# Attention products turned round: v as the stationary operand, 64-row score products, and maxima read straight from PSUM

## The chip, the cores and the metric

The program runs on one core of one Trainium2 chip, as one launch. The metric is the device time of one execution in microseconds. A core has five instruction queues: TensorE (matmuls, written PE in the profile, its weight loads PEld), VectorE (DVE), ScalarE (ACT), GpSimd (POOL) and SyncE (SP), which mostly issues DMAs. Each queue runs its instructions in order; semaphores hold one queue until another has done its part.

## The reference

Attention with rotary position encoding over 4 batches, 8 heads, 576 positions and 64 dimensions, then a mixture of 8 experts with one expert for each of 2304 tokens, then a dense feed-forward layer. The change touches the attention alone:

```
q_rot, k_rot = rotate(q), rotate(k)
scores = (1 / sqrt(64)) * q_rot @ k_rot.T          # 32 times 576 x 576
scores = scores - max(scores, over keys)
attn = exp(scores);  attn = attn / (sum(attn, over keys) + 1e-9)
out = attn @ v                                     # 576 x 64 for each head
x = out, heads side by side: 2304 x 512            # input of the experts
```

All inputs and outputs are fp32.

## The kernel before

**Pairs of heads.** The 32 heads are handled as 16 pairs, `p` = 0 to 15, four pairs to a batch. Head `e` (0 or 1) of a pair has its 64 dimensions on partitions 64e to 64e+63. `load` brings q and k, `rope` rotates them (six tensor operations a pair, on GpSimd except where `OFF` names them for VectorE), `hi` and `lo` split each rotated value into two 16-bit halves, and `stack` lays the halves out by DMA so that 128 rows hold both halves of one head.

**Scores twice.** `sc` (L279) multiplies queries (stationary) with keys (moving) for the row maximum: eight tiles of 128 queries, four for each head, and a ninth that holds the last 64 queries of both heads. A tile has 576 columns in two PSUM banks of 288. ScalarE copies one bank to SBUF (L294), and VectorE scans it against the other bank, so that the last element is the maximum (`sc_max`, L305). `m_split` (L319, L329) negates the maxima into a small matrix, `m_turn` (L335 to L341) turns it by two matmuls, copies it out and writes it by two DMAs from SP's queue into the stacked operands as one more row. `st` (L351, L352) then computes the scores again, transposed (keys on partitions, queries along the columns), with that row taking the maximum off, in two matmuls for each of two column blocks. `exp` (L354) writes the nine tiles to `P`, in fp32.

**Product with v.** `p_lo` (L360) subtracts from each fp32 weight its upper 16 bits, read in place as bf16, which gives a lower half in fp16; some tiles do this on GpSimd, as `OFF['pool...']` lists, the others on VectorE. `pv` (L375 to L377) has the weights as stationary operand (128 keys x 128 queries) and v as the moving one: 64 columns, and a column of 0.25 whose product is the row sum. Three products of halves for each of five key blocks and five query blocks and two heads make 150 matmuls a pair. Each head has an accumulator bank of its own (`obank`, two in turn). `epi` (L386 to L399) adds 1e-9, inverts the sum and multiplies. `v_load`, `v_hi` and `v_lo` bring and split v once a batch. `r_hi`, `r_lo` and the functions after them route the result to the experts.

**Buffers.** Six PSUM banks are three pairs (`pair`, L140), given out in turn to `sc`, `st`, `m_turn` and the router's products. Before a pair is given out again, `Turns` emits the maximum that is still to read it (L136).

**Order.** Every function is entered with a due time (`add`, L60); `emit` sorts all by it, and that is the order of each engine's instructions. A pair of heads is nine units apart from the next (`z = 9 * p`, one unit for each `st` tile). `sc` of a pair runs 15.7 units ahead of its first `st`, `m_turn` about 5 ahead, `pv` from 10.4 to 18.5 units behind. `OFF` holds small shifts of these due times by function, tile and pair. The expert visits start at unit 144.6, while pair 15 is at unit 135 to 154.

Of the kernel before, what the change touches and what calls it, by code (L numbers as in the profile page):

```python
# [44 lines left out]
def kernel(ctx: ExitStack, tc: tile.TileContext, qk, vp, cs, cf, tid, emb, tau, w1, w2, wi, wo, out, tag=None):  # L45
# [63 lines left out]
    for name, size in (  # L109
# [3 lines left out]
    ):  # L113
        off[name], top = top, top + size
# [14 lines left out]
    class Turns:  # L129
# [62 lines left out]
    qkt, hlt, mtp, pt, ot, xt, vh, vl, v32 = ({} for _ in range(9))  # L192
# [37 lines left out]
    def v_load(b, g):  # L230
        v32[b, g] = v32t()
        nc.sync.dma_start(out=v32[b, g].rearrange("p a d -> p (a d)"), in_=vp[b][:, 576 * g:576 * g + 576])

    def v_hi(b, g):
        if g == 0:
            vh[b] = at(f"v{b % 2}", F16, 36, 65)
            vl[b] = at(f"v{b % 2}", F16, 36, 64, add=4704)
            nc.gpsimd.memset(vh[b][:, :, 64:65], 0.25)
        nc.scalar.activation(vh[b][:, 9 * g:9 * g + 9, 0:64], v32[b, g], AF.Copy, scale=64.0)

    def v_lo(b, g):
        r = slice(9 * g, 9 * g + 9)
        nc.vector.scalar_tensor_tensor(vl[b][:, r], v32.pop((b, g)), 64.0, vh[b][:, r, 0:64], op0=ALU.mult, op1=ALU.subtract)
# [29 lines left out]
    def warm(n):  # L273
        t = bank(obank(), 512)
# [4 lines left out]
    def sc(p, i):  # L279
        after(("stack", p))  # L280
        d = D4[p % 4]
        t = pair()
        for c in OFF.get('c1', (0, 1)):
            cc = slice(288 * c, 288 * c + 288)
            if i < 8:
                e, q0 = i // 4, (i % 4) * 128
                nc.tensor.matmul(t[:, c, 0:288], lhsT=d[:, e, 0, q0:q0 + 128], rhs=d[:, e, 2, cc], start=True, stop=True)  # L287
            else:
                for e in range(2):
                    nc.tensor.matmul(t[64 * e:64 * e + 64, c, 0:288], lhsT=d[:, e, 0, 512:576], rhs=d[:, e, 2, cc], start=True, stop=True)  # L290
        m = sE[(9 * p + i) % 15]
        sct[p, i] = t
        pair.due[(pair.n - 1) % 3] = p, i
        nc.scalar.copy(m, t[:, 1, 0:288])  # L294

    sE = [at("et", F16, 288, add=576 * s) for s in range(15)]
    sct = {}

    def sc_max(p, i):
# [3 lines left out]
        m = sE[(9 * p + i) % 15]  # L303
# [3 lines left out]
    def m_split(p, i):  # L307
        mv = at("et", F16, 15, 288)[:, :, 287]
        mh = MH1[p % 2]
        after(*[("sc_max", p, k) for k in (range(4), range(4, 8), (8,), ())[i]])  # L310

        def put(c, s, n):
            while n:
                s %= 15
                k = min(n, 15 - s)
                if p in OFF.get('msA', ()):
                    nc.scalar.activation(mh[:, c:c + k], mv[:, s:s + k], AF.Copy, scale=-1.0)
                else:
                    nc.vector.tensor_scalar(mh[:, c:c + k], mv[:, s:s + k], -1.0, None, op0=ALU.mult)  # L319
                c, s, n = c + k, s + k, n - k  # L320

        if i == 0:
            put(0, 9 * p, 4)
        elif i == 1:
            put(5, 9 * p + 4, 4)
        elif i == 2:
            put(4, 9 * p + 8, 1)
        else:
# [950 lines left out]
```

## Time and profile before

| | |
|---|---|
| median of 3 runs | 1074.34 us (1073.21 to 1080.97) |
| the profiled execution | 1081.06 us |
| its span, first to last instruction | 1079.2 us |
| TensorE busy, share of the span | 900.1 us, 83% |
| VectorE | 809.6 us, 75% |
| GpSimd | 607.7 us, 56% |
| ScalarE | 549.6 us, 51% |
| mean granted TensorE clock | 0.91 |

The span is one execution on the chip. A matmul's busy time holds its drain, which overlaps the next matmul, so a busy TensorE need not be at its peak; what a matmul costs in a row of them is the distance of the starts. The granted clock is 1.00 at 2.4 GHz and 0.5 at 1.2 GHz; a stretch's figure is the mean. Attention fills the first third of the span, the experts and the feed-forward layer the rest, so shares over the whole span say little on attention.

### The profile page before, as it was taken

Reading aid. Unit: us, or ns where it says so; the run is one execution under the profiler, and the core shown is the slowest. Engines: PE = TensorE matmul, PEld = TensorE weight load, DVE = VectorE, ACT = ScalarE, POOL = GpSimd, SP = SyncE. Lnnn points to the kernel's source line nnn. Section 1 sums busy time; section 2 is a strip of 40 time slices with the busy share of each in tenths; the row PEclk is TensorE's granted clock in tenths of the full one; section 3 lists DMA queues with packets and bytes.
Section 4 is the critical chain, followed back from the end, with each engine's and each line's share of the span. In section 5 each row is a group of like instructions: output and inputs, shape, how many; then the busy total and the mean of one; then the engine's idle time right before and its main releaser. Section 6 shows DMA issues by size and latency. Waiting matters only on the chain. (4 is left out here: it accounts for less than half of the span.)

```text
span 1079.2 us, 25502 instructions
## 1 busy us (share of the span) xinstructions
PE 900.1 (83%) x9622; PEld 702.8 (65%) x9622; DVE 809.6 (75%) x1265; ACT 549.6 (51%) x982; POOL 607.7 (56%) x665
## 2 busy tenths in 40 slices
PE   2577788777788899899968897369899999999994
PEld 1255556545566687677645573258688888888884
DVE  8898998999986846666899887896656656655751
ACT  2454564546455633555776544544555555554540
POOL 6585685677543713233234655567667757657650
PEclk8588887889798989899989998699899999999998
DMA  6644337446342744979999655210112022012000
GB/s 222 187 133 133 89 94 165 153 125 127 104 108 50 227 101 139 297 209 284 327 319 281 194 144 157 81 41 11 50 40 60 21 41 60 21 41 60 21 20 20
DMA packets 128426, 133.73 MB, mean 124 GB/s; under 512 B 67736, under 2 KB 104600, under 8 KB 128288
## 3 DMA queue, kind: packets, MB, share of 16 engines
q1 hardware_dynamic: 119648, 103.75, 35.8%
q0 software_dynamic: 8352, 27.62, 7.8%
q8 instruction: 78, 1.28, 0.5%
q10 hardware_dynamic: 288, 0.59, 0.2%
q14 instruction: 60, 0.49, 0.1%
HBM read 86.36 MB, written 16.17 MB: 95 GB/s over the span
## 5 line engine op out<-in xcount | busy, mean ns | idle before, releaser
L1047 PE MATMUL banks<-arena 128*128 128x256 f16 x576 | 160.1, 278 | 30.9 <-ACT arena L1062 25.9
L1048 PE MATMUL banks<-arena 128*128 128x256 f16 x576 | 160.2, 278 | 0.0
L1049 PE MATMUL banks<-arena 128*128 128x256 f16 x576 | 160.1, 278 | 0.0
L354 ACT ACTIVATE arena<-banks 128x576 f32<-128x576 f32 x144 | 93.4, 652 | 115.2 <-PE banks L352 114.9
L1082 DVE TENSOR_TENSOR arena<-arena 128x896 f16<-128x896 f32 x72 | 80.2, 1114 | 88.8 <-ACT arena L1078 84.1
L1099 PE MATMUL banks<-arena 128*128 128x256 f16 x504 | 138.1, 274 | 4.0 <-DVE arena L1114 4.0
L1100 PE MATMUL banks<-arena 128*128 128x256 f16 x504 | 138.2, 274 | 0.0
L1101 PE MATMUL banks<-arena 128*128 128x256 f16 x504 | 138.2, 274 | 0.0
L967 PE MATMUL banks<-arena 128*128 128x128 f16 x704 | 125.9, 225 | 9.6 <-DVE arena L940 7.3
L965 PE MATMUL banks<-arena 128*128 128x128 f16 x704 | 126.1, 225 | 8.7 <-DMA arena<-arena 8.7
L1078 ACT ACTIVATE arena<-arena 128x896 f16<-128x896 f32 x71 | 67.5, 950 | 127.8 <-POOL arena L1075 124.3
L966 PE MATMUL banks<-arena 128*128 128x128 f16 x704 | 126.1, 225 | 0.0
L305 DVE TENSOR_TENSOR_SCAN arena<-banks,arena 128x288 f16<-128x288 f32 x144 | 106.5, 747 | 19.2 <-ACT arena L294 18.2
L377 PE MATMUL banks<-arena 128*128 128x65 f16 (+1 forms) x800 | 114.5, 202 | 6.9 <-DVE arena L360 6.1
L375 PE MATMUL banks<-arena 128*128 128x65 f16 (+1 forms) x800 | 115.8, 205 | 0.0
L360 POOL TENSOR_TENSOR arena<-arena 128x576 f16<-128x576 f32 x48 | 65.2, 1362 | 89.6 <-ACT arena L354 80.6
L376 PE MATMUL banks<-arena 128*128 128x64 f16 (+1 forms) x800 | 115.1, 202 | 0.0
L351 PE MATMUL banks<-arena 128*128 128x288 f16 (+1 forms) x320 | 89.1, 319 | 20.3 <-DVE arena L305 17.1
L1072 POOL TENSOR_TENSOR arena<-arena 128x256 f32<-128x256 f32 x67 | 54.5, 813 | 86.7 <-DVE arena L1069 86.7
L360 DVE TENSOR_TENSOR arena<-arena 128x576 f16<-128x576 f32 x96 | 96.0, 1004 | 2.4 <-ACT arena L354 2.4
L375 PEld LDWEIGHTS <-arena 128*128 128x128 bf16 (+1 forms) x800 | 80.0, 103 | 25.4 <-issue 10.1
L287 PE MATMUL banks<-arena 128*128 128x288 f16 x256 | 65.3, 333 | 32.7 <-DVE arena L305 23.7
(236 smaller groups left out, 2737.3 us busy)
## 6 DMA issues: line engine op xcount, KB each, us to landing
arena<-in_w_dram SPq DMA_DIRECT2D x64, 512.0 KB
arena<-in_qk_dram SPq DMA_DIRECT2D x30, 576.0 KB
arena<-in_wi_dram SPq DMA_DIRECT2D x16, 512.0 KB
arena<-in_wo_dram SPq DMA_DIRECT2D x32, 256.0 KB
arena<-arena SPq DMA_DIRECT2D x32, 216.0 KB
xreg<-arena POOLq DMA_DIRECT2D x25, 260.0 KB, 4.3
arena<-in_vp_dram SPq DMA_DIRECT2D x16, 288.0 KB
arena<-arena SPq DMA_DIRECT2D x32, 144.0 KB
```

The source lines that it names most:

```text
L360: eng.tensor_tensor(PLO[:, r], P32[:, r], PHB[:, r], op=ALU.subtract)
L375: nc.tensor.matmul(o[:, qt, :], lhsT=PHB[r, q], rhs=vh[b][r, vi], start=kt == 0, stop=False)
L376: nc.tensor.matmul(o[:, qt, 0:64], lhsT=PHB[r, q], rhs=vl[b][r, vi], start=False, stop=False)
L965: nc.tensor.matmul(o[:, fc], lhsT=w[:, 0, a], rhs=x[:, k], start=k == 0, stop=False)
L966: nc.tensor.matmul(o[:, fc], lhsT=w[:, 0, a], rhs=x[:, 4 + k], start=False, stop=False)
L967: nc.tensor.matmul(o[:, fc], lhsT=w[:, 1, a], rhs=x[:, k], start=False, stop=k == 3)
L1047: nc.tensor.matmul(o[:, v], lhsT=wih[k][:, f0:f0 + 128], rhs=z[:, :, k], start=k == 0, stop=False)
L1048: nc.tensor.matmul(o[:, v], lhsT=wih[k][:, f0:f0 + 128], rhs=z[:, :, 4 + k], start=False, stop=False)
L1049: nc.tensor.matmul(o[:, v], lhsT=wil[k][:, f0:f0 + 128], rhs=z[:, :, k], start=False, stop=k == 3)
L1099: nc.tensor.matmul(y, lhsT=a, rhs=b, start=u + f + n == 0, stop=False)
L1100: nc.tensor.matmul(y, lhsT=a, rhs=w[:, 1, WB[i - 1]], start=False, stop=False)
L1101: nc.tensor.matmul(y, lhsT=q[:, 1, f, GB[i - 1]], rhs=b, start=False, stop=u + f == 4 and n == len(m) - 1)
```

## The change

- The **score products** for the maximum (`sc`) contract over 64 rows, the upper halves of q and k alone, instead of 128. The tiles of the two heads are computed in one call, matmul by matmul in turn, from rows 0 to 63 and 64 to 127.
- The **maximum** (`sc_max`) is one reduction over both banks, negated, written straight into the small matrix. The copy by ScalarE and three of the four parts of `m_split` are gone.
- `m_turn`'s two DMAs are issued by ScalarE's queue instead of SP's.
- **`pv`** has v as the stationary operand, 64 columns for each head, so that head 0 writes PSUM partitions 0 to 63 and head 1 partitions 64 to 127; the weights are the moving operand, 576 queries in blocks of 256 and 320. Key blocks 0, 1 and 2 (`KF`) are multiplied in fp32; blocks 3 and 4 (`KH`) in three products of halves as before. The row sums come from a stationary of 32 columns of 0.25, in four strips of 32 partitions, in what is left of the two banks. The work is cut by key blocks, and each is due while the pair's `st` still runs.
- `p_lo` is left with tiles 3, 7 and 8; of these 3 and 8 are on GpSimd and 7 on VectorE, for every pair.
- Both heads share the two accumulator banks. `o_out` copies them to SBUF, `o_turn` turns them by eight fp32 transposes into a `pair`, and `epi` reads from there, for both heads at once.
- v is loaded in five parts a batch instead of four; three stay in fp32 in place, two are split.
- Due times: `pv` runs 3.6 to 10.9 units behind the first `st`, and what follows a pair (`y`) 12.9 instead of 19.6. The order of `st` tiles alternates between the heads. In `OFF`, the shifts of `p_lo`, `pv`, `epi`, `m_split`, `m_turn`, `v_hi`, `v_lo` and `sc_max` and the lists `pool1` to `pool15` and `poolz` are gone. `r_acc_t` and `r_acc` are now also emitted before their PSUM pair is given out again, and the router of batch 2 is due 10.2 instead of 7.2 units after `y`.

```diff
+    KF, KH = (0, 1, 2), (3, 4)
+    LT = [4 * e + kt for kt in KH if kt < 4 for e in range(2)] + [8]
-    obank = Turns([banks[:, 6], banks[:, 7]])
+    obank = banks[:, 6:8]
...
-    def sc(p, i):
+    def sc(p, n):
...
+            for e in range(2):
+                a, ce = slice(64 * e, 64 * e + 64), c if n < 4 else (c + e) % 2
+                o = two[e][:, ce, 0:288] if n < 4 else two[e][a, ce, 0:288]
+                nc.tensor.matmul(o, lhsT=d[a, e, 0, q0:q0 + (128 if n < 4 else 64)], rhs=d[a, e, 2, 288 * ce:288 * ce + 288], start=True, stop=True)
-        nc.scalar.copy(m, t[:, 1, 0:288])
...
-        nc.vector.tensor_tensor_scan(m, t[:, 0, 0:288], m, -3e38, op0=ALU.max, op1=ALU.max)
+        nc.vector.tensor_reduce(out=MH1[p % 2][:, c:c + 1], in_=t[:, :, 0:288], op=ALU.max, axis=AX.XY, negate=True)
...
-        nc.sync.dma_start(out=d[64:65, 0, 1], in_=ms[0:5])
-        nc.sync.dma_start(out=d[0:1, 1, 1], in_=ms[5:10])
+        nc.scalar.dma_start(out=d[64:65, 0, 1], in_=ms[0:5])
+        nc.scalar.dma_start(out=d[0:1, 1, 1], in_=ms[5:10])
...
+    def pv(p, kt):
...
+        if kt in KF:
+            w = [vm[i2][:, KF.index(kt), 2 * (p % 4) + e] for e in range(2)]
+            terms = [[(w[e], P32[:, (9 * p + tiles[e][0]) % RP]) for e in range(2)]]
+            ones = [[(one32, P32[:, (9 * p + tiles[e][0]) % RP]) for e in range(2)]]
+        else:
...
+                for t, x in zip(terms, ((h, ph), (h, pl), (l, ph))):
+                    t.append(x)
+                for t, x in zip(ones, (ph, pl)):
+                    t.append((one16[a], x))
+        for c in range(2):
+            for n, t in enumerate(terms):
+                for e in range(2):
+                    w, x = t[e]
+                    nc.tensor.matmul(o[64 * e:64 * e + 64, c, 0:QC[c].stop - QC[c].start], lhsT=w, rhs=x[:, QC[c]], ...)
+        for c in range(2):
+            q0, m = QS[c]
+            for n, t in enumerate(ones):
+                for e in range(2):
+                    w, x = t[e]
+                    for h in range(2):
+                        r = 64 * e + 32 * h
+                        nc.tensor.matmul(o[r:r + 32, c, 512 - m:512] if c else o[r:r + 32, c, 256:384], lhsT=w, rhs=x[:, q0 + 128 * h:q0 + 128 * h + m], ...)
+    def o_out(p):
+        s = osb[p % 2]
+        nc.scalar.copy(s[:, 0, 0:384], obank[:, 0, 0:384])
+        nc.scalar.copy(s[:, 1], obank[:, 1])
+    def o_turn(p):
...
+        for k, a in enumerate((0, 128, 512, 640, 768, 256, 832, 960)):
+            nc.tensor.transpose(t[:, k], s[:, a:a + 128], cft[:, 0:128])
...
+            nc.vector.tensor_tensor(x, t[:, 0:5]..., ert.pop(p).to_broadcast([128, 5, 2, 64]), op=ALU.mult)
...
+        for n in range(5):
+            add(u + w * 2 * n, sc, p, n)
...
+            add(z + i, st, p, 4 * (i % 2) + i // 2 if i < 8 else 8)
+        for kt, t in zip(PVO, (3.6, 5.5, 7.5, 9.6, 10.9)):
+            add(z + t, pv, p, kt)
+        add(z + 11.3, o_out, p)
+        add(z + 12.6, o_turn, p)
...
-        b, y = p // 4, z + 19.6
+        b, y = p // 4, z + 12.9
```

## Rows read from the trace of the kernel before

**Rows 1.** The exponentials' line: count, duration ns min/median/max, first and last start.

```profile
L354 ACT ACTIVATE arena<-banks x144: 624/651/693, 44.4 to 372.2; 128x576 f32<-128x576 f32 x144
```

**Rows 2.** Stretches: busy us and instructions of each engine, granted clock, DMA share, GB/s.

```profile
107.00:329.00 222.00, 175.02 (x2296) 126.74 (x2294) 206.50 (x348) 120.86 (x263) 143.85 (x101) 0.85 0.45 117
329.00:372.00 43.00, 40.62 (x664) 31.54 (x661) 33.73 (x89) 27.24 (x53) 22.07 (x21) 0.92 0.51 145
372.00:405.00 33.00, 28.55 (x443) 24.45 (x441) 17.66 (x29) 11.73 (x24) 9.98 (x7) 0.90 0.54 123
...
800.00:840.00 40.00, 40.00 (x369) 35.85 (x367) 23.58 (x33) 20.85 (x36) 29.51 (x43) 1.00 0.15 41
```

**Rows 3.** Waits, 107 to 329: who waited for whom, us, times, longest.

```profile
ACT arena L354 <- PE banks L352: 73.8, 68, 5.4
PE banks L335 <- DVE MH L319: 17.2, 10, 2.9
```

**Rows 4.** Groups on TensorE, 107 to 329: busy us, mean ns, idle before, releaser.

```profile
L351 PE MATMUL banks<-arena 128*128 128x288 f16 x161 | 49.8, 320 | 11.7 <-DVE arena L305 10.3 <-DMA arena<-arena 0.6 <-DVE r L386 0.6
L287 PE MATMUL banks<-arena 128*128 128x288 f16 x170 | 42.5, 321 | 8.4 <-DVE arena L305 8.1
```

**Rows 5.** Groups on VectorE, 107 to 329.

```profile
L305 DVE TENSOR_TENSOR_SCAN arena<-banks,arena 128x288 f16<-128x288 f32 x97 | 72.2, 748 | 12.5 <-ACT arena L294 12.2
L360 DVE TENSOR_TENSOR arena<-arena 128x576 f16<-128x576 f32 x63 | 61.7, 981 | 0.0
...
L243 DVE SCALAR_TENSOR_TENSOR arena<-arena 128x576 f16<-128x576 f32 x10 | 15.5, 1550 | 0.0
L319 DVE TENSOR_SCALAR MH<-arena 128x4 f16<-128x4 f16 x17 | 11.6, 682 | 0.0
...
L399 DVE TENSOR_TENSOR arena<-banks,r 128x320 f32<-128x320 f32 x20 | 9.8, 490 | 0.6
```

**Rows 6.** Groups on ScalarE: copies of scores, 107 to 329; a 512-column PSUM read.

```profile
L294 ACT CAST arena<-banks 128x288 f16<-128x288 f32 x97 | 38.2, 396 | 7.7 <-PE banks L287 5.9 <-PE banks L290 0.7
...
L1060 ACT ACTIVATE arena<-banks 128x512 f32<-128x512 f32 x72 | 42.8, 594 | 26.3 <-PE banks L1049 17.9 <-issue 4.4 <-DVE arena L1015 2.4
```

**Rows 7.** SP's queue: its longest wait, 107 to 329; one issue (start, us).

```profile
SPq L340 <- ACT arena L294: 108.2, 9, 18.2
...
121.55 0.75 SPq L340 DMA_DIRECT2D arena<-ms  x1
```

**Rows 8.** Groups on GpSimd, 107 to 329.

```profile
L360 POOL TENSOR_TENSOR arena<-arena 128x576 f16<-128x576 f32 x28 | 38.0, 1358 | 58.2 <-ACT arena L354 50.0 <-DMA arena<-arena 8.2
L254 POOL TENSOR_TENSOR arena<-arena 128x576 f32<-128x576 f32 x19 | 32.1, 1687 | 0.7
```

**Rows 9.** TensorE in order of time from 209.56: start us, us, line.

```profile
209.56 0.19 PE L377 MATMUL banks<-arena 64*128 64x65 f16 x1
209.69 0.30 PE L351 MATMUL banks<-arena 128*128 128x288 f16 x1
209.82 0.29 PE L352 MATMUL banks<-arena 128*128 128x288 f16 x1
209.94 0.29 PE L351 MATMUL banks<-arena 128*128 128x288 f16 x1
210.06 0.29 PE L352 MATMUL banks<-arena 128*128 128x288 f16 x1
...
210.43 0.19 PE L375 MATMUL banks<-arena 128*128 128x65 f16 x1
210.46 0.19 PE L376 MATMUL banks<-arena 128*128 128x64 f16 x1
```

**Rows 10.** The same around a tile of column halves, from 194.93.

```profile
194.93 0.28 PE L352 MATMUL banks<-arena 128*128 128x288 f16 x1
...
195.15 0.14 PEld L290 LDWEIGHTS <-arena 128*64 128x64 f16 x4 [0.23 <-issue]
195.15 0.44 PE L290 MATMUL banks<-arena 128*64 128x288 f16 x4
```

More of the change, by code (lines that the diff above doesn't have):

```diff
@@ L135, in __call__ @@
             if i in self.due:
-                sc_max(*self.due.pop(i))
+                f, *a = self.due.pop(i)
+                f(*a)
             self.n += 1
@@ L191 @@
         nc.vector.memset(t, 0.0)
-    qkt, hlt, mtp, pt, ot, xt, vh, vl, v32 = ({} for _ in range(9))
+    qkt, hlt, xt = ({} for _ in range(3))
     et = at("P", F32, DM, add=23040)[0:8]
@@ L277, in warm @@
             nc.tensor.matmul(t, lhsT=z[:, 0:128], rhs=z[:, 0:512], start=True, stop=True)
-    def sc(p, i):
+    def sc(p, n):
         after(("stack", p))
         d = D4[p % 4]
-        t = pair()
-        for c in OFF.get('c1', (0, 1)):
[L284 to L293, printed above, removed]
-        nc.scalar.copy(m, t[:, 1, 0:288])
-    sE = [at("et", F16, 288, add=576 * s) for s in range(15)]
+        if n < 4:
+            two = []
+            for e in range(2):
+                two.append(pair())
+                sct[p, 4 * e + n] = two[e]
+                pair.due[(pair.n - 1) % 3] = sc_max, p, 4 * e + n
+            q0 = 128 * n
+        else:
+            two, q0 = [pair()] * 2, 512
+            sct[p, 8] = two[0]
+            pair.due[(pair.n - 1) % 3] = sc_max, p, 8
+        for c in OFF.get('c1', (0, 1)):
+            for e in range(2):
+                a, ce = slice(64 * e, 64 * e + 64), c if n < 4 else (c + e) % 2
+                o = two[e][:, ce, 0:288] if n < 4 else two[e][a, ce, 0:288]
+                nc.tensor.matmul(o, lhsT=d[a, e, 0, q0:q0 + (128 if n < 4 else 64)], rhs=d[a, e, 2, 288 * ce:288 * ce + 288], start=True, stop=True)
     sct = {}
@@ L302, in sc_max, with m_split @@
         done.add(('sc_max', p, i))
-        m = sE[(9 * p + i) % 15]
         t = sct.pop((p, i))
-        nc.vector.tensor_tensor_scan(m, t[:, 0, 0:288], m, -3e38, op0=ALU.max, op1=ALU.max)
[L307 to L328, printed above, removed]
-            nc.vector.tensor_copy(MH2[p % 2][:, 9:10], mh[:, 4:5])
+        c = i if i < 4 else i + 1 if i < 8 else 4
+        nc.vector.tensor_reduce(out=MH1[p % 2][:, c:c + 1], in_=t[:, :, 0:288], op=ALU.max, axis=AX.XY, negate=True)
+    def m_split(p):
+        after(*[("sc_max", p, k) for k in range(9)])
+        nc.vector.tensor_copy(MH2[p % 2][:, 9:10], MH1[p % 2][:, 4:5])
     def m_turn(p):
         mh, m2 = MH1[p % 2], MH2[p % 2]
-        after(*[("m_split", p, i) for i in range(4)])
+        after(("m_split", p))
         tp = bank(pair(), 1, 128)[0:10, 0]
@@ L362, in pv @@
[L362 to L377 removed]
+        nc.scalar.activation(P32[:, (9 * p + i) % RP].rearrange("p (c n) -> p c n", c=2), t[:, :, 0:288], AF.Exp, scale=2.0)
@@ L423, in r_logits_t @@
             lgp[b, 0] = bank(pair(), 5, 8)
+            pair.due[(pair.n - 1) % 3] = r_acc_t, b
         x, o = xT.pop((b, t, 0)), lgp[b, 0]
@@ L430, in r_acc_t @@
     def r_acc_t(b):
+        if (b, 0) not in lgp:
+            return
         lac[b] = small.tile([128, 5, 8], F32, name="l", tag="l")
@@ L449, in r_logits @@
         b, k = p // 4, p % 4
-        o = bank(pair() if p < NP - 3 else rbank(), 5, 8)
+        o = bank(pair() if p < NP - 2 else rbank(), 5, 8)
         lgp[p] = o
+        if p < NP - 2:
+            pair.due[(pair.n - 1) % 3] = r_acc, p
         xh, xl = xT.pop((p, 0)), xT.pop((p, 1))
@@ L459, in r_acc @@
         b, k = p // 4, p % 4
+        if p not in lgp:
+            return
         if k == 0:
@@ L782 @@
                 add(y + 4.5 + d, r_logits, p)
-                add(y + 5.0 + d, r_acc, p)
+                add(y + 5.6 + d, r_acc, p)
         else:
@@ L1161 @@
         if j < 6:
[L1162 removed]
+            add(zg0 + 3.4 + .9 * j if j < 5 else max(zg4 + .1, ZV + ZU * 4.3 + .1), x_gather, j)
         else:
```

162 lines of the change are left out of this document (87 added, 75 removed), and 2 rows, old and new, of the table SZ.

## Prediction

> **What bounds the kernel now.** I read the engines by stretch first, then the largest groups of each engine in the steady stretch, then the order of matmuls in time, then the waits. The change touches attention alone. Its softmax exponentials, nine to a pair of heads, begin at 44.4 and the last begins at 372.2 us [rows 1]. From 107 to 329 us 91 of them fall (counted in the group of the line), so 222 us hold 10.1 pairs: **22.0 us a pair**. In that stretch VectorE is busy 206.5 of 222 us, 20.4 us a pair, TensorE 175 (with overlapping drains counted) at a granted clock of 0.85, GpSimd 143.9 and ScalarE 120.9 [rows 2]. VectorE is the bound: the exponentials wait 73.8 us for products, m_turn's products wait 17.2 us for the negated maxima [rows 3], and st and sc wait 10.3 and 8.1 us for PSUM that a maximum still reads [rows 4]. From 329 us on this is over: TensorE is busy 40.6 of 43 us, then 28.6 of 33, while VectorE falls to 33.7 and 17.7 [rows 2]; there pairs 14 and 15 share TensorE with the first expert visits.
>
> **VectorE, per pair.** The subtraction p_lo ran 63 times in the stretch, 6.1 us a pair; the default now leaves it tile 7 alone, 0.98 us: -5.1. The negations of m_split go, at least 11.6 us of the stretch: -1.15. v_lo takes 768 instead of 2304 columns a batch: two thirds of 15.5 us, -1.0 [rows 5]. The maximum reads 576 columns straight from PSUM instead of scanning 288 beside a copied 288. No reduction of that size is in the trace; a PSUM operation of 320 columns takes 490 ns, and at that pace 576 take 880. I take the scan's own 748 ns, between the two and also from PSUM; the ends are -2.3 and +1.2 us a pair. The two epilogue multiplies of 320 columns become one of 640: even. Left: **20.4 - 7.25 = 13.2 us**.
>
> **ScalarE.** The copy of half a score tile goes: 38.2 us in the stretch, -3.8 a pair. o_out adds 384 and 512 columns from PSUM; 512 took 594 ns, so about 1.04 [rows 6]. The two DMAs of m_turn move here from SP, where one issue takes 0.75 us: +1.5 [rows 7]. 12.0 - 3.8 + 1.04 + 1.5 = 10.7 us, and the exponential queued behind those issues is covered by ScalarE's own waiting for products (73.8 us in ten pairs); without that cover it is 1.5 us a pair. On SP they had stood at the head of the queue for 108.2 us, with the next pair's loads and stacking behind them [rows 7]; that goes, and I count it at nothing, since st waited only 0.6 us for a DMA in the stretch [rows 4]. One more v load a batch goes through a queue that was idle that long: nothing.
>
> **GpSimd.** Two p_lo a pair instead of 28 in 10.1: 3.8 becomes 2 x 1.358 = 2.7, so 14.2 becomes 13.2 us; six rope operations of up to 1.69 us stay [rows 8].
>
> **TensorE, per pair.** Prices at full clock [rows 9]: four matmuls of 288 columns start 0.12 to 0.13 us apart, 0.123, which is 0.427 ns a column; those of 65 columns are 0.03 apart; where the array changes from 64 rows to 128, the step after a 65-column matmul is 0.13, so a change of shape costs 0.10. Four column halves (64 outputs each, 288 columns) all ran in 0.44 us; one alone lasts 0.28, and in a row each would add 0.123, 0.65 in all: they go two and two, side by side [rows 10]. Before: st 32 x 0.123 + 4 x 0.123 = 4.4, sc 2.2, pv 150 x 0.03 = 4.5, 26 changes of shape 2.6, m_turn 0.1: **13.8 us**, and 15.8 with its columns at the clock of 0.85.
> After: st is the same, 4.4. The score products use 64 rows a head; two heads side by side give 10 x 0.123 = 1.2, and without overlap 2.5, no more than before; I take 1.2 since column halves overlap. The two 16-bit blocks stream 3 x 576 + 2 x 320 columns each, two heads (and four row-sum strips) side by side: 2 x 2368 x 0.427 ns = 2.0. For fp32 the trace has no matmul at all. The low end is one pass a column, 3 x 896 x 0.427 = 1.15 us; then VectorE and GpSimd bound a pair at 13.2, with waits 13.6, and the time would be 957 us. The high end is four passes, as an exact product of two numbers in halves takes four products (the old code makes three and drops the smallest), with nothing side by side: 3 x 9728 columns = 12.5. I take four passes with the heads side by side and the strips in twos: 3 x (576 + 640) x 4 x 0.427 = **6.2**; with the strips in fours too it is 4.6. The eight fp32 transposes of o_turn cost 0.44 (one pass) to 1.75 (four), taken 1.1. Changes of shape: 25, 2.5. Sum **17.6 us**.
> The Trainium skill's page "FP8 and Floating Point Precision" (TensorE Precision Notes) says that true fp32 makes four passes, high and low parts crosswise. By that the sum stays at 17.6; no run here shows it.
>
> **The sum.** TensorE becomes the longest by 4.4 us over VectorE and GpSimd. Where it was the bound before, the clock was 1.00 (40 of 40 us busy) [rows 2], so I price it at full clock and add 0.4 us of waits: 18.0 us a pair. Pairs 0 to 13: 14 x (22.0 - 18.0) = -56. Pairs 14 and 15 run where TensorE is already short, and pay 2 x (17.6 - 13.8) = +7.6. Start of the kernel: nothing (between -3.6, nine copies of 0.4 us less before the first maxima are whole, and +1.5 for the DMAs on ScalarE). Router and table work are put earlier by their due times, behind the same early visits: nothing; if the cover fails, at most the 4.5 us that TensorE idled from 372 to 405. The experts and the feed-forward part run no differently and only shift. **-48 us.** The profiled execution took 1081.06 us (span 1079.2 and 1.9 around it), 6.7 over the median of 1074.34, so 1033 on its own scale and **1026 on the median**.
>
> **Rivals.**
> *All strips side by side, transposes in one pass* (chance 0.25). TensorE 15.3 and 15.7 with waits, GpSimd and VectorE 13.2 below it: 14 x 6.3 - 2 x 1.5 = -85, 989 us. For it: the column halves overlap two and two [rows 10]. Against: nothing with four strips, and nothing in fp32, is there.
> *The waits stay* (0.14). Both heads now share one accumulator, so the next pair's pv stands in TensorE's queue behind o_out: an exponential ahead (0.65), the copies (1.04) and the way there, about 1.9 us, against 1.4 us of st, sc and m_turn in between: 0.5. If the waits for maxima (17.2 us) and for PSUM (10.3 + 8.1) keep their 1.7 and 1.8 us a pair too, a pair takes 21.6: 14 x -0.4 + 7.6 = +2, 1076 us (1060 to 1085). Against it: these waits came from a full VectorE.
> *fp32 heads one after the other* (0.11, the slower side). If a multi-pass fp32 matmul doesn't let its neighbour in, the three fp32 blocks cost 12.5 us and TensorE 24.5, with waits 24.9: 14 x 2.9 + 2 x 10.7 = +62, 1136 us. It decides from 22.0 us a pair on, that is from 10.2 us for these blocks, four fifths of the serial cost.
> *Weight loads come to light* (0.03). The 92 narrow stationaries of a pair each load in 0.10 to 0.14 us as the narrow ones before did [rows 10]; if none hid, 9.5 us more: 14 x 5.5 + 2 x 13.3 = +104, 1178 us. Against: the four loads of the narrow tiles lay within 0.14 us, under their matmuls.
> The Trainium skill's page "TensorEngine Tiling (Array Packing)" (Restrictions and Gotchas) says that column tiling excludes the fast weight load, which is the mechanism of this rival; the trace's narrow loads do not show it as time.
> *Forecast* (0.47): 1005 to 1050.
>
> **The numbers.** Under 1% (about 11 us) no difference can be told. Faster: 0.47 + 0.25 + 0.03 of the waits = 0.75. Same: 0.09 of the waits. Slower: 0.02 + 0.11 + 0.03 = 0.16. The range reaches from the full overlap, 988, to where most of the waits are in, 1078; outside lie the two dear cases (0.14), the end of the waits, and the one-pass price below 988, together about 0.2.
>
> **What would show it.** Right: VectorE under 70% of the attention stretch; 144 reductions of about 0.75 us; 16 p_lo on VectorE and 32 on GpSimd; fp32 matmuls of the two heads starting within a few ns; clock near 1.0; first to last exponential about 270 us instead of 328. Wrong: fp32 matmuls of one head starting only when the other's end, TensorE idle ahead of pv or m_turn, or an exponential that comes as seldom as now with TensorE half idle.

## The result: no faster, a little slower

The changed kernel took 1084.82 us (1080.56 to 1089.9), the kernel before, run beside it, 1076.36: a ratio of **1.0087 [1.0062, 1.0111]**. Forecast were 1026 us and a range of 988 to 1078. The profiled execution has a span of 1086.7 us (1079.2 before). The stages of the changed kernel, with the columns of [rows 2]:

```profile
107.00:329.00 222.00, 186.93 (x2185) 102.39 (x2182) 144.07 (x233) 101.42 (x198) 122.00 (x95) 0.94 0.49 123
329.00:372.00 43.00, 37.85 (x491) 22.36 (x490) 17.20 (x61) 16.17 (x30) 14.38 (x14) 0.92 0.45 128
372.00:405.00 33.00, 23.12 (x313) 16.10 (x310) 15.28 (x22) 17.48 (x32) 3.31 (x3) 0.95 0.27 74
```

VectorE did fall, from 206.5 to 144 of 222 us, GpSimd from 143.9 to 122, ScalarE from 120.9 to 101. And still the exponentials, which count the pace, come hardly faster. Their line, which answers to [rows 1]:

```profile
L360 ACT ACTIVATE arena<-banks x144: 631/651/682, 43.4 to 387.6; 128x576 f32<-128x576 f32 x144
```

The pace is read from the first exponential of pair 3 to that of pair 13, ten pairs, first before and then in the changed kernel:

```profile
107.32 0.67 ACT L354 ACTIVATE arena<-banks 128x576 f32<-128x576 f32 x1
329.16 0.65 ACT L354 ACTIVATE arena<-banks 128x576 f32<-128x576 f32 x1 [0.23 <-PE banks L352]
...
107.30 0.65 ACT L360 ACTIVATE arena<-banks 128x576 f32<-128x576 f32 x1
325.14 0.65 ACT L360 ACTIVATE arena<-banks 128x576 f32<-128x576 f32 x1 [1.30 <-PE banks L359]
```

A pair takes 21.78 us (22.18 before; the forecast counted 22.0). Pair 13 begins 4.0 us earlier than before, but the last exponential starts 15.4 us later: pairs 13 to 15 take 62.5 us instead of 43.1. The first products of the dense layer start at 673.0 instead of 665.7, and the end comes 7.5 us later. The pace is one execution's: a second trace of the changed kernel (the control run below) has 21.46, so differences of 0.3 us in it tell nothing.

The groups of 107 to 329 us that answer to [rows 4, 5, 6, 8]: busy us, mean ns, idle time before them and its releaser.

```profile
L358 PE MATMUL banks<-arena 128*128 128x288 f16 x163 | 44.4, 291 | 16.8 <-ACT arena L360 13.7 <-DVE MH L332 1.7 <-DVE MH L336 1.3
...
L396 PE MATMUL banks<-arena 128*64 128x320 f32 x120 | 23.9, 480 | 0.0
L396 PE MATMUL banks<-arena 128*64 128x256 f32 x120 | 22.3, 454 | 0.0
...
L332 DVE TENSOR_REDUCE MH<-banks 128x1 f16<-128x576 f32 x97 | 70.2, 754 | 56.5 <-PE banks L322 56.5
...
L372 DVE TENSOR_TENSOR arena<-arena 128x576 f16<-128x576 f32 x10 | 9.6, 961 | 2.9 <-ACT arena L360 2.9
...
L411 ACT COPY arena<-banks 128x512 f32<-128x512 f32 x10 | 6.0, 601 | 0.0
...
L372 POOL TENSOR_TENSOR arena<-arena 128x576 f16<-128x576 f32 x21 | 24.1, 1146 | 80.0 <-ACT arena L360 80.0
```

The new maximum costs what it was taken at (754 ns; 748 taken). VectorE now stands 56.5 us waiting for score products, and GpSimd 80.0 us for exponentials: neither bounds anything. The waits of the stretch, in the columns of [rows 3], first the other engines', then TensorE's own:

```profile
ACT arena L360 <- PE banks L359: 114.7, 65, 6.6
...
DVE MH L332 <- PE banks L322: 56.5, 43, 3.4
...
PE banks L358 <- ACT arena L360: 13.7, 33, 1.0
...
PE banks L342 <- DVE MH L336: 8.8, 5, 2.3
PE banks L467 <- DMA arena<-arena: 3.9, 2, 2.2
PE banks L420 <- DVE MH L332: 2.8, 6, 0.5
```

Everyone waits for TensorE, and TensorE waits too: 35.1 of 222 us pass between the end of one matmul and the start of the next (47.0 before). Before, nearly all its waits were for VectorE; now the largest is st (L358) for the exponential. Where it falls is seen in TensorE's order of time (start, us, idle before and releaser in brackets), the view of [rows 9]:

```profile
272.20 0.42 PE L358 MATMUL banks<-arena 128*128 128x288 f16 x1
272.42 0.45 PE L359 MATMUL banks<-arena 128*128 128x288 f16 x1
...
273.13 0.42 PE L322 MATMUL banks<-arena 64*128 64x288 f16 x4
273.93 0.28 PE L358 MATMUL banks<-arena 128*128 128x288 f16 x1 [0.39 <-ACT arena L360]
...
274.51 1.19 PE L396 MATMUL banks<-arena 128*64 128x256 f32 x8
275.63 0.75 PE L404 MATMUL banks<-arena,one 128*32 128x128 f32 x16
276.32 0.30 PE L358 MATMUL banks<-arena 128*128 128x288 f16 x1
276.45 0.29 PE L359 MATMUL banks<-arena 128*128 128x288 f16 x1
...
276.91 0.42 PE L322 MATMUL banks<-arena 64*128 64x288 f16 x4
277.72 0.28 PE L358 MATMUL banks<-arena 128*128 128x288 f16 x1 [0.39 <-ACT arena L360]
...
282.14 0.95 PE L396 MATMUL banks<-arena 128*64 128x256 bf16 x12
283.02 0.47 PE L404 MATMUL banks<-arena,one 128*32 128x128 bf16 x16
283.42 0.30 PE L358 MATMUL banks<-arena 128*128 128x288 f16 x1
...
289.42 0.22 PE L342 MATMUL banks<-c,MH 128*10 128x128 f16 x1 [1.83 <-DVE MH L336]
...
290.23 1.94 PE L420 MATMUL banks<-cft,arena 128*128 128x128 f32 x8 [0.53 <-DVE MH L332]
```

A score step now takes two of the three PSUM pairs at once. The st tile behind it needs the third, which the exponential of the st before is still reading: 0.39 us here, 13.7 us in 33 such waits over the stretch. At 289.42 m_turn waits 1.83 us for the last maxima, at 290.23 o_turn for one more. Behind these waits the eight transposes take 1.94 us, at a granted clock of 0.50; without a wait they take 1.13 (below). Over the stretch TensorE spends 25.7 us on matmuls at the lower of its two clock levels (0.5). There st's matmuls start 0.22 us apart (272.20 to 272.42), at the upper one 0.13 (276.32 to 276.45). Each of the stretch's six low spans begins at one of its six longest waits (1.63 to 2.29 us), or within 2.5 us behind it.

### The profile page after: what moved, and what is told of

Read it like the earlier page. It is cut to its first block, busy times and chain, and to the rows that moved or that the text cites. A ratio compares the mean times of both kernels' runs of the same rounds, so it can differ in the third digit from the quotient of the medians.

```text
span 1086.7 us, 24670 instructions
## 1 busy us (share of the span) xinstructions
PE 923.2 (85%) x9398; PEld 666.0 (61%) x9398; DVE 708.3 (65%) x1091; ACT 517.9 (48%) x874; POOL 558.9 (51%) x646
## 5 line engine op out<-in xcount | busy, mean ns | idle before, releaser
L332 DVE TENSOR_REDUCE MH<-banks 128x1 f16<-128x576 f32 x144 | 103.9, 753 | 75.2 <-PE banks L322 74.8
L1017 PE MATMUL banks<-arena 128*128 128x128 f16 x704 | 123.4, 223 | 7.4 <-DVE arena L990 6.2
L1015 PE MATMUL banks<-arena 128*128 128x128 f16 x704 | 123.6, 223 | 0.0
L1016 PE MATMUL banks<-arena 128*128 128x128 f16 x704 | 123.6, 223 | 0.0
L372 POOL TENSOR_TENSOR arena<-arena 128x576 f16<-128x576 f32 x32 | 36.7, 1147 | 145.3 <-ACT arena L360 145.2
L396 PE MATMUL banks<-arena 128*64 128x256 f32 (+9 forms) x768 | 97.0, 381 | 7.3 <-DVE arena L372 4.2
L358 PE MATMUL banks<-arena 128*128 128x288 f16 (+1 forms) x320 | 80.1, 298 | 23.9 <-ACT arena L360 17.3
L990 DVE SCALAR_TENSOR_TENSOR arena<-arena 128x1024 f16<-128x1024 f32 x64 | 84.8, 1365 | 9.3 <-ACT arena L988 7.7
L1053 PE MATMUL banks<-arena 128*128 128x512 f16 x176 | 69.2, 393 | 15.7 <-DVE arena L990 11.5
L1098 PEld LDWEIGHTS <-arena 128*128 128x128 f16 x576 | 57.3, 99 | 38.9 <-issue 31.5
L359 PE MATMUL banks<-arena 128*128 128x288 f16 (+1 forms) x320 | 79.1, 294 | 0.0
L997 POOL DMA_INDIRECT arena<-xreg,gidx x25 | 29.1, 1165 | 94.8 <-DMA xreg<-arena 80.4
```

The costliest lines, as they stand in the source:

```text
L332: nc.vector.tensor_reduce(out=MH1[p % 2][:, c:c + 1], in_=t[:, :, 0:288], op=ALU.max, axis=AX.XY, negate=True)
L396: nc.tensor.matmul(o[64 * e:64 * e + 64, c, 0:QC[c].stop - QC[c].start], lhsT=w, rhs=x[:, QC[c]], start=first and n == 0, stop=end and n = ...
L1015: nc.tensor.matmul(o[:, fc], lhsT=w[:, 0, a], rhs=x[:, k], start=k == 0, stop=False)
L1016: nc.tensor.matmul(o[:, fc], lhsT=w[:, 0, a], rhs=x[:, 4 + k], start=False, stop=False)
L1017: nc.tensor.matmul(o[:, fc], lhsT=w[:, 1, a], rhs=x[:, k], start=False, stop=k == 3)
L1098: nc.tensor.matmul(o[:, v], lhsT=wih[k][:, f0:f0 + 128], rhs=z[:, :, 4 + k], start=False, stop=False)
```

## The experiments

Each ratio is against the kernel before, timed alongside; the changed kernel stands at 1.0087. "Pace" is pair 3 to pair 13, as above.

**The maximum alone.** The kernel before, with the new score products, reduction and negation (sc, sc_max, m_split) and all else old.

```diff
-        nc.scalar.copy(m, t[:, 1, 0:288])
...
-        nc.vector.tensor_tensor_scan(m, t[:, 0, 0:288], m, -3e38, op0=ALU.max, op1=ALU.max)
+        nc.vector.tensor_reduce(out=MH1[p % 2][:, c:c + 1], in_=t[:, :, 0:288], op=ALU.max, axis=AX.XY, negate=True)
```

> The kernel before with the new maximum alone: 64-row score products for both heads in turn, one reduction straight from PSUM, no copy by ScalarE, one part of m_split; pv, p_lo, epi and m_turn's queue as before. Theory A (before, VectorE at 20.4 us a pair was the bound; the turned pv is what made TensorE the bound): VectorE loses 1.2 to 1.6 us a pair and its waits for the copy, a pair takes 20 to 21 us, 10 to 25 us faster than the kernel before. Rival (the new maximum itself, two PSUM pairs taken at once, makes the waits): st's waits for PSUM grow and it is no faster than before.

Measured: 0.998 [0.995, 1.001], pace 21.67. The stretch 107 to 329:

```profile
107.00:329.00 222.00, 167.64 (x2372) 117.92 (x2371) 206.54 (x320) 95.24 (x178) 145.86 (x102) 0.85 0.45 118
```

VectorE stays full (206.54), and ScalarE is freed by 25 us of which nothing is seen. TensorE's idle time in the stretch grew from 47.0 to 54.4 us, as the rival had it: st waits 14.8 us for maxima (10.3 before), the score products 12.1 (8.1). So this half of the change alone gains nothing that can be told. The other half, the turned pv with the old maximum, was not run alone.

**m_turn's DMAs back on SP, and p_lo of the last pairs on VectorE.**

```diff
-        nc.scalar.dma_start(out=d[64:65, 0, 1], in_=ms[0:5])
-        nc.scalar.dma_start(out=d[0:1, 1, 1], in_=ms[5:10])
+        nc.sync.dma_start(out=d[64:65, 0, 1], in_=ms[0:5])
+        nc.sync.dma_start(out=d[0:1, 1, 1], in_=ms[5:10])
```

> The changed kernel with m_turn's two DMAs back on SP's queue. If the two issues on ScalarE (counted at 1.5 us a pair) delay exponentials that TensorE then waits for: 3 to 10 us faster than the changed kernel, ratio 0.999 to 1.006. If, as the prediction had it, ScalarE's slack covers them and SP's queue has room: the same, 1.007 to 1.010. If the next pair's loads then stand behind them on SP: slower than 1.010.

Measured: 1.0103 [1.0062, 1.0143], pace 22.30: not told apart from the changed kernel, and if anything slower. The queue of these DMAs is not what ate the gain.

```diff
-OFF = {'MX': 0.8, 'pool': (3, 8), ...
+OFF = {'MX': 0.8, 'pool': (3, 8), 'pool14': (), 'pool15': (), ...
```

> The changed kernel, with p_lo of pairs 14 and 15 on VectorE instead of GpSimd. Theory A (TensorE's queue sets the pace, and its waits are what ate the gain; two of them, 0.4 and 2.8 us near 364 and 369 us, are pv waiting for p_lo on a GpSimd that also issues the gathers): pv's waits for GpSimd vanish, the steady stretch stays at 22 us a pair, the end comes 3 to 8 us earlier than in the changed kernel (ratio to the kernel before 1.001 to 1.006). Theory C (the whole loss is in the last two pairs, which no longer fit their old lists): the end comes 10 us or more earlier, ratio 0.999 or less.

Measured: 1.0071 [1.0044, 1.0099], not told apart from the changed kernel. It tests this place in the changed kernel's TensorE order:

```profile
363.94 0.83 PE L396 MATMUL banks<-arena 128*64 128x256 f16 x10 [0.39 <-POOL arena L372]
...
368.75 1.44 PE L396 MATMUL banks<-arena 64*64 64x256 f16 x10 [2.76 <-POOL arena L372]
```

The waits are real. With these tiles on VectorE the last exponential started 3.8 us earlier (383.8), but what is left of that at the end is not told from nothing.

**More work for TensorE.** The fp32 row sums streamed a second time, against a stationary of zeros.

```diff
-            ones = [[(one32, P32[:, (9 * p + tiles[e][0]) % RP]) for e in range(2)]]
+            ones = [[(k, P32[:, (9 * p + tiles[e][0]) % RP]) for e in range(2)] for k in (one32, nil32)]
```

> The changed kernel with the row sums of the three fp32 blocks streamed a second time through a stationary of zeros, which adds nothing to the result: 2.07 us more TensorE work a pair (3 x 0.69). Theory A (TensorE's work and waits both lie on the path): a pair takes about 24 us, the end comes 28 to 36 us later than in the changed kernel, ratio 1.034 to 1.042. Rival B (turnaround of PSUM sets the pace): the extra work fills waits, st's waits for exponentials shrink, and the end comes less than 12 us later.

Measured: 1.0269 [1.0212, 1.0325], some 20 us over the changed kernel. The row sums of an fp32 block now take 1.23 us to the next st instead of 0.69:

```profile
207.62 0.43 PE L406 MATMUL banks<-arena,one 128*32 128x128 f32 x8
207.86 0.40 PE L406 MATMUL banks<-arena,nil 128*32 128x128 f32 x8
...
208.85 0.30 PE L360 MATMUL banks<-arena 128*128 128x288 f16 x1
```

That is 1.6 us a pair at the upper clock (2.07 had been expected), 26 us over 16 pairs, of which 20 are paid. The pace went to 22.84, 1.05 us more (1.38 against the control's 21.46). Neither theory's figures came out: most of the added work is paid, but not all. TensorE is neither the whole bound nor free.

**One wait taken away.** m_split and m_turn of pairs 1 to 13 two units later, when the maxima are there.

```diff
-        add(u + 10 * w, m_turn, p)
+        add(u + (12 if 0 < p < 14 else 10 * w), m_turn, p)
```

> The changed kernel with m_split and m_turn of pairs 1 to 13 two units later, and nothing else. Theory A (each wait in TensorE's queue is paid): the 8.8 us that m_turn waits for the maxima between 107 and 329 go, 8 to 13 us over all pairs, ratio 0.997 to 1.002. Rival (that wait only covers another one): st waits longer for the next PSUM pair, the ratio stays within 1.005 to 1.010.

Measured: 0.9993 [0.9969, 1.0017], pace 21.87 (21.78). TensorE's waits from 107 to 329:

```profile
PE banks L358 <- ACT arena L360: 15.6, 31, 2.4
PE banks L420 <- DVE MH L332: 8.4, 4, 2.4
```

The ratio is the one that Theory A forecast (0.997 to 1.002), and lies below the changed kernel's interval. But the gain does not come from where that theory had it. In 107 to 329 us m_turn's 8.8 us are gone, and o_turn waits 8.4 instead of 2.8, st 15.6 instead of 13.7: there the wait moved, and the pace stayed. What is gained is gained earlier: pair 3 begins at 100.3 us instead of 107.3 (107.7 in the control), and from 44 to 107 us o_turn's waits fall from 4.9 to 2.3 us and m_turn's from 2.1 to 1.0, at a granted clock of 0.95 instead of 0.86. So a wait of TensorE that is taken away can be worth its time, or can come back at the next step.

**The order, and nothing but the order.** Each score step is put between the products and the row sums of a key block (`pv` cut into `pv` and `pvs`), so that the row sums, 0.7 us of an fp32 block and 0.4 us of a 16-bit one, stand between it and the next st; m_turn goes 3.7 units ahead of its pair, o_turn behind another pair's st. pv, the maxima and the epilogue move with them, and the shifts of pairs 14 and 15 (`u@14`, `u@15`) go. Every instruction of the changed kernel is there: the counts by engine, operation and shape are the same.

```diff
+        su = [u + w * 2 * n for n in range(5)] if not p else [z + t for t in (-13.6, -11.6, -9.6, -7.6, -6.6)]
...
-        add(u + 10 * w, m_turn, p)
+        add(u + 10 * w if not p else z - 3.7, m_turn, p)
...
-        for kt, t in zip(PVO, (3.6, 5.5, 7.5, 9.6, 10.9)):
+        for kt, t in zip(PVO, (4.2, 6.2, 8.2, 10.2, 11.2)):
             add(z + t, pv, p, kt)
+            add(z + t + .4, pvs, p, kt)
...
-        add(z + 12.6, o_turn, p)
+        add(z + 13.1, o_turn, p)
```

> The changed kernel with another order on TensorE and the same work: each pv is cut into products and row sums, and the score products go between the two, so that no st stands right behind a score product that took the last PSUM pairs; m_turn later, o_turn ahead of pv. Theory A (TensorE's queue is the path: 18.5 us of work and 3.5 us of waits a pair): most of the waits of st for an exponential (13.7 us in 107 to 329) and of m_turn for the maxima (8.8) go, a pair takes 19 to 20 us instead of 22, the end comes 25 to 45 us earlier. Rival B (PSUM turnaround between ScalarE, VectorE and TensorE sets the pace, whatever the order): the waits turn up at other instructions and a pair still takes 21.5 to 22.5 us.

Measured: **0.9623 [0.9569, 0.9676]**, 1033.42 us; once more beside the last runs (label e17_order_again), 0.9633 [0.9587, 0.9679].

> The reordered kernel once more, unchanged, on the chip of the three others: 0.957 to 0.968 as the first time, about 1033 us.

TensorE's order of time in this kernel (L411 are the row sums, L427 the transposes), and its stretch 107 to 329:

```profile
211.73 1.13 PE L427 MATMUL banks<-cft,arena 128*128 128x128 f32 x8
212.79 1.19 PE L396 MATMUL banks<-arena 128*64 128x256 f32 x8
213.91 0.42 PE L322 MATMUL banks<-arena 64*128 64x288 f16 x4
214.26 0.75 PE L411 MATMUL banks<-arena,one 128*32 128x128 f32 x16
214.94 0.30 PE L358 MATMUL banks<-arena 128*128 128x288 f16 x1
```

```profile
107.00:329.00 222.00, 199.30 (x2568) 116.82 (x2570) 147.19 (x286) 114.34 (x221) 129.16 (x103) 0.97 0.56 143
```

No row of these five has a bracket: nothing waits. (The last 46 us of the stretch hold pair 13 and what follows it here.) The pace:

```profile
94.36 0.65 ACT L360 ACTIVATE arena<-banks 128x576 f32<-128x576 f32 x1 [1.91 <-PE banks L359]
283.16 0.65 ACT L360 ACTIVATE arena<-banks 128x576 f32<-128x576 f32 x1 [0.90 <-PE banks L359]
```

It is 18.88 us a pair (18.87 in the second run). From 107 to 300 us, a pair has 16.9 us of occupied TensorE and 2.0 of waits, where the changed kernel has 18.3 and 3.5. Of the 1.4 us less of occupied TensorE, 0.8 is the clock: matmuls at the lower level fall from 25.7 to 12.5 us in that stretch, and at the upper one they start half as far apart. The order also saves changes of shape: 21.3 a pair instead of 24.9 from pair 3 to 13, which at the forecast's 0.10 us each is an estimated 0.4 us.

**Which move carries it?** The score steps behind the whole pv alone; the turning steps alone; both together without the cut.

```diff
+        su = [u + w * 2 * n for n in range(5)] if not 0 < p < 14 else [z - 17.95 + t for t in (3.6, 5.5, 7.5, 9.6, 10.9)]
```

> The changed kernel with the score products of pairs 1 to 13 moved behind the products with v (uncut), where they stand before an st tile in the shipped order; the turning steps stay. Theory A (each wait of TensorE is a cost of its own): st's wait for the exponential before it, 13.7 us in 10.2 pairs, goes: 1.3 us a pair, 14 pairs, 19 us less, 1066 us or a ratio of 0.99. Theory B (the waits are one loop; a single link moved shows up elsewhere): within 5 us of the changed kernel, ratio 1.005 to 1.013, with the wait at another place. Theory C (the place of the score products carries most of the gain of the reordered kernel): 1045 to 1060, 0.97 to 0.985.

Measured: 1.0039 [1.0016, 1.0061], pace 21.78. TensorE's waits, 107 to 329:

```profile
PE banks L358 <- DVE MH L332: 10.5, 28, 1.0
PE banks L396 <- DVE arena L372: 8.9, 8, 2.5
PE banks L342 <- DVE MH L332: 6.5, 8, 1.7
...
PE banks L358 <- ACT arena L360: 0.4, 1, 0.4
```

```diff
+        add(z - 3.7 if 0 < p < 14 else u + 10 * w, m_turn, p)
...
+        add(z + 12.6 if p > 13 else z + 13.1, o_turn, p)
```

> The changed kernel with m_turn of pairs 1 to 13 two units later and o_turn and epi of pairs 0 to 13 half a unit later, behind the next pair's work that covers the copies; the score products and pv stay. Theory A: their waits (8.8 and 2.8 us in 10.2 pairs, 1.1 us a pair) go: 16 us less, ratio 0.995. Theory B: same as the changed kernel, 1.005 to 1.013, with st's wait for the exponential grown by what the turns no longer wait. Theory C (the turns carry the gain): 0.97 to 0.985.

Measured: 0.997 [0.9941, 1.0], pace 20.83. The waits:

```profile
PE banks L358 <- ACT arena L360: 11.2, 24, 2.0
PE banks L358 <- DVE arena L439: 11.1, 9, 1.7
```

```diff
-            add(z + t + .4, pvs, p, kt)
+            add(z + t + .1, pvs, p, kt)
```

> The kernel of e2 with the row sums put back right behind the products, so that the score products stand between a whole pv and the next st. If the place of the score products does it (st must not need a PSUM pair that they have just taken): st's waits come back, mostly for maxima now, 0.4 to 1.0 us at four places a pair, and a pair takes 20 to 22 us, 1050 to 1080 us in all. If moving pv, m_turn and o_turn did it and the cut nothing: within 5 us of e2.

Measured (the reordered kernel uncut): 0.9751 [0.9703, 0.9798], pace 19.47. In the first, st's wait for the exponential is as good as gone (13.7 to 0.4) and the same time stands at the maxima, at p_lo and at m_turn. In the second the turning steps' waits are gone and st waits 11.1 us for the epilogue's read (L439) of the PSUM pair. Counted in pace, the score steps alone give 0.0, the turning steps alone 0.95, both 2.3, with the cut 2.9 us a pair. By the ratio, against the changed kernel's 1.0087, the score steps alone give 0.005, hardly told apart, the turning steps alone 0.012, about what their waits cost, as Theory A had it; both give 0.034, with the cut 0.046. Alone, the moves are made for pairs 1 to 13 and against the shipped due times of pv, which the reordered kernels have 0.3 to 0.7 units later; that later pv was not run alone, and part of the difference may be its. The moves are worth more together than apart. That would fit one loop of waits through the three PSUM pairs, where a link that goes alone lets the next one tighten; no run shows the loop itself.

**Is TensorE the bound then?** The reordered kernel with the same second row sums as above.

> The reordered kernel (e2_order) with the fp32 row sums streamed a second time against a stationary of zeros: 2.07 us more of TensorE's work a pair. If TensorE is the bound there, nearly all of it is paid: 16 x 1.8 to 2.07 = 29 to 33 us over the reordered kernel, about 0.990. If waits still set the pace as in the shipped order, where 20 us were paid: 10 to 20 us, 0.972 to 0.981.

Measured: 0.9792 [0.9748, 0.9836], 19 us over the unloaded reordered kernel (1059.73 against 1040.67). The added rows cost TensorE the same 1.6 us a pair as in the shipped order (an fp32 block's row sums again take 1.23 us instead of 0.68). By the pace 1.42 us of it are paid (18.87 to 20.29), against 1.05 to 1.38 in the shipped order; by the whole time 19 of 26 us, against 20 of 26. So the two orders do not differ clearly in this: in both most of the added work is paid and not all, and the forecast's "TensorE becomes the longest" holds for its work, not for a full engine.

**Attempts to go on from there**, all with p_lo of pairs 14 and 15 on VectorE (`'pool14': (), 'pool15': ()`).

> The reordered kernel with p_lo of pairs 14 and 15 on VectorE. If the two waits of pv for GpSimd were worth anything once the order is right: 2 to 5 us faster than the reordered kernel, ratio 0.957 to 0.961. If the tail is hidden behind the first expert weights anyway: the same, 0.962.

Measured: 0.9592 [0.9552, 0.9632], not told apart from the reordered kernel (1040.15 us, and 1033.42 the reordered, each beside other runs of before). These two, and the one with the later router products below, are the fastest versions found, and all three beat both kernels.

```diff
-    KF, KH = (0, 1, 2), (3, 4)
+    KF, KH = (0, 1), (2, 3, 4)
```

> The reordered kernel with the tail of the run before, and key block 2 in halves instead of fp32: per pair 0.54 us less TensorE work (1.81 against 1.27), two p_lo more on VectorE (about 1.9 us; it was busy two thirds). Theory A (TensorE's queue is still the path): 5 to 9 us faster than the run before. Rival B (VectorE's and ScalarE's turnaround sets the pace now): the two p_lo delay maxima, and it is the same or slower.

Measured: 0.9672 [0.9626, 0.9719], pace 19.26: 9 us slower than the run before, which was timed beside it (1049.18 against 1040.15), though a 16-bit block costs TensorE 1.28 us and an fp32 block 1.81. st's waits for maxima grew to 19.8 us in 107 to 329 (6.1 in the reordered kernel). I took two more p_lo on VectorE for the reason and moved them:

```diff
-OFF = {'MX': 0.8, 'pool': (3, 8), ...
+OFF = {'MX': 0.8, 'pool': (2, 6, 3, 8), ...
```

> The kernel of e7 (reordered, two fp32 blocks), with the two added p_lo tiles on GpSimd instead of VectorE. If e7 lost because those p_lo stood ahead of the maxima in VectorE's queue (st waited 17.2 us for maxima between 107 and 300, against 5.8 in the reordered kernel): that wait falls back to 4 to 8 us and the time to that of e5 or 5 to 8 us below it. If it lost because pv of block 2 now waits for a p_lo at all: pv or its row sums wait for GpSimd, and it is no better than e7.

Measured: 0.9754 [0.9707, 0.9801], no better, and st's waits for maxima stand at 24.2 us; so that was not the reason, and what lengthens this wait stays open.

```diff
-                    add(y + (11 if b < B - 2 else 9) + .001 * t, r_logits_t, b, t)
+                    add(y + (14 if b < B - 2 else 9) + .001 * t, r_logits_t, b, t)
...
```

> The kernel of e5 with the router's products of batches 0 and 1 three units later, so that the DMA transposes they wait for have landed (3.7 us in one such wait, 4.6 us in two between 107 and 300). TensorE's queue as the path: 3 to 6 us faster than e5. If that wait hides behind others: the same.

Measured: 0.9618 [0.957, 0.9666] (`r_acc_t` and the router's later steps are moved by the same three units). From 107 to 300 us the router's wait for its DMA went from 4.6 us to nothing, st's waits for maxima grew from 6.8 to 12.0, and the time stayed: the wait moved once more.

**The changed kernel again**, as a control.

> The changed kernel as it is, as the yardstick on this chip for the runs beside it: 1.006 to 1.011 of the kernel before.

Measured: 1.0121 [1.0079, 1.0163], which overlaps 1.0087 [1.0062, 1.0111]. The pace is 21.46, with the same 3.4 us of waits a pair and 18.6 us instead of 25.7 at the lower clock level.

## Why the prediction was wrong, step by step

- **VectorE, GpSimd, ScalarE: right within a tenth.** At 10.2 pairs in 107 to 329 us, 144.07 is 14.1 us a pair (13.2 forecast), 122.0 is 12.0 (13.2), 101.4 is 9.9 (10.7). m_turn's DMAs, moved off SP [rows 7], take 0.69 us of ScalarE's queue each, and moving them back gained nothing that can be told.
- **TensorE's work: right in sum.** 186.9 us occupied are 18.3 a pair; its part at the lower clock, 25.7 us, would take 12.9 at the upper one, so 17.1 at full clock against 17.6 forecast. An fp32 block is 1.81 us from the first product to the st behind it (274.51 to 276.32), 2.07 and two shape changes of 0.10 forecast: the four row-sum strips of 32 columns run all side by side, so here the cheaper end (strips in fours) holds, the first half of the first rival. A 16-bit block is 1.28 us (282.14 to 283.42), about 1.2 forecast. Eight transposes are 1.06 us from start to next start (1.1 forecast; the first rival's one pass would be 0.44). A score step of both heads takes 0.35 us with its change of shape (213.91 to 214.26): two and two side by side, as forecast.
- **The rival "fp32 heads one after the other" falls.** The two heads' fp32 records start 7 ns apart (274.513 and 274.520). The Trainium skill's page "FP8 and Floating Point Precision" (TensorE Precision Notes) has four passes for true fp32. The trace agrees in price: each matmul leaves two records, the second of 256 columns 0.216 us before the next matmul, 0.84 ns a column against the 0.427 of one 16-bit pass, so the price of two passes in each record. (The rival's sum of 24.5 us is 0.6 more than its terms, 17.6 - 6.2 + 12.5; nothing hangs on it.)
- **"Weight loads come to light" falls.** The fp32 stationaries load in 137 ns (median), and the groups of L396 have no idle time before them. By the Trainium skill's page "TensorEngine Tiling (Array Packing)" (Restrictions and Gotchas) column tiling excludes the fast weight load; here the loads lie under their matmuls.
- **The step that failed: "so I price it at full clock and add 0.4 us of waits: 18.0 us a pair".** Measured are 3.4 us of waits (35.1 us in 10.2 pairs) and 1.3 for the clock that falls beside the longest of them: 17.1 + 1.3 + 3.4 = 21.8, the pace of 21.78. The full clock was read from a stage in which TensorE alone was full (40 of 40 us); the 0.4 had no row behind it. Here no engine is full: TensorE's matmuls stand in one fixed order with steps that need another engine's answer at once. I had taken the old waits for a full VectorE's; with VectorE a third idle they came back behind other releasers.
- **The rival that came true, "the waits stay"** (21.6 us a pair, 1060 to 1085 us), had the size, at a chance of 0.14. Its reasons hold in part: m_turn still waits for maxima, but no wait of pv for the copies of the accumulator (L410, L411) is listed in the stretch, and the largest wait, st behind a score step that takes two PSUM pairs, stood in no sentence of mine, though the change computes a score step for both heads in one call.
- **That order and not work was the cause is shown** by the reordered kernel: 18.9 us a pair and 0.962 of the kernel before, near the 18.0 and 0.955 forecast, with the same instructions. What each of its moves is worth is only in part told apart.
- **The signs.** Four of the six things that the forecast named as showing it right came true: VectorE at 65% of the stretch, 144 reductions of 0.75 us, 16 p_lo on VectorE and 32 on GpSimd, fp32 starts 7 ns apart. They test the work, which the rival of the waits shares. The two that test the time failed: a clock of 0.94, and 344 us from the first to the last exponential instead of 270.
- **Where the time was lost.** Pair 13 was forecast to begin 52 us earlier and begins 4.0 earlier: 48 of the 55 us that the forecast missed by are lost by then.
- **Pairs 14 and 15: +7.6 us forecast, too little.** Pairs 13 to 15 take 19.4 us more than before, of which 8 are regained by the start of the dense layer. One wait in it (GpSimd's p_lo) was tried and does not account for it; the rest was not traced.

## What to carry to other kernels

When the bounding engine is relieved, the time need not fall to the next engine's busy sum: look up, for each step in that engine's fixed order, whose answer it needs and how much other work stands between. A step that takes two of three buffers at once leaves the step behind it waiting for the last reader of the third; put independent work between the two, about as long as what is left of that reader. Try such moves together: here two of them alone gained 0.5% and 1.2%, and together, with pv a little later, 3.3%.

## What the hardware showed beyond that

- fp32 products on narrow column tiles overlap as 16-bit ones do: the records of four strips of 32 columns start 6 to 7 ns apart (275.634 to 275.654), and sixteen records of 128 and 192 columns end within 0.75 us.
- An fp32 transpose of 128 columns costs 0.13 us at a granted clock of 1.00 (eight in 1.06 us), and the eight behind two waits, at 0.50, took 1.94 us instead of 1.13.
- A reduction of 576 elements straight from two PSUM banks takes 754 ns, as long as the scan of 288 from PSUM beside 288 from SBUF (748, [rows 5]).
